# Approximate exponentials on VectorE as four shifted linear terms, in a statically ordered attention kernel

## The chip, the cores and the metric

The kernel runs on one core of a Trainium2 chip. The metric is the device time of one execution in microseconds (us). Executions of the same kernel differ by 1 to 3% here from the fastest to the slowest, mostly with the granted clock of TensorE (the share of its full speed that the profile shows as granted): a run over 1.5% above the fastest of its kernel in the same series is called slow and is left out of the ratios.

## The reference

Two attention layers read their own inputs and write side by side. Part A is multi-query attention with 32 heads of width 16, one shared key and value head, and 2048 queries and keys. Part B is a linear attention whose feature map is a pair of softmaxes over 16 values.

```python
# part A
q = (x @ wq).reshape(B, S, H, Dh)            # S = 2048, H = 32, Dh = 16
k = x @ wk;  v = x @ wv                      # one head for all
p = softmax(einsum("bhqd,bkd->bhqk", q, k) * Dh ** -0.5)
a = einsum("bhqk,bkd->bhqd", p, v) ... @ wo
# part B: phi = [softmax(pq), softmax(-pq)], kv = phi_k^T v, o = phi_q kv / (phi_q z)
return concatenate([a, b], axis=-1)          # (1, 2048, 1024), bf16
```

Part A needs 32 x 2048 x 2048 = 134 million exponentials, which is what the kernel is about.

## The kernel before

The scores are computed transposed, keys on partitions. Four heads are handled together (a head group of 512 queries: 32 such groups). A **quad** is one group against 128 keys: four 128x512 tiles of scores, one for each head. There are 32 x 16 = 512 quads. Each is turned into exponentials by one of two engines:

- ScalarE reads two or three score tiles at a time from PSUM and writes exp in bf16 (line L1620, tile `f_PT`). TensorE then multiplies a quad by the values with four matmuls that sit side by side in the array (L1662; in the trace they start 3 ns apart).
- VectorE approximates exp. It evicts each score tile as a 16-bit integer that is the bit pattern of an fp16 number near exp (L1711, `f_Z`), and refines it with two masks and two products (`f_U`, `f_E`, `f_C`). TensorE adds the three terms up with weights K: twelve matmuls (L1760).

```python
def bits():                                   # VectorE, once a tile: 128x512 f32 -> int16
    v.tensor_scalar(out=Z[:, p, h, :], in0=ps[:, bank, :], scalar1=Z1, scalar2=Z0, op0=mult, op1=add)
# ... then, once a pair of tiles (128x1024):
U = (Z & 0x3ff) | 0x3c00                      # tensor_scalar, int16
E = Z & 0x7c00                                # tensor_scalar, int16
C = Z.f16 * U.f16                             # tensor_tensor, fp16
C = C * U.f16                                 # tensor_tensor, fp16
# TensorE:  ACC += K0*V^T E + K1*V^T Z + K2*V^T C      (4 heads side by side, 3 terms)
```

The order of the instructions on every engine is fixed when the kernel is built. A greedy list scheduler keeps a clock for each engine with durations written in the program, picks the next job by priority, and emits it. VectorE gets a quad whenever its queue is short and the head group has at least `AHEAD` quads left; ScalarE gets the rest.

```python
def dq_ok(self):                              # may VectorE take another score tile?
    if self.dbusy > 3.2 or self.dz_out or (...ring of Z is full...):
        return False
    return self.dn % 4 != 0 or self.dve_quad() is not None    # a group with >= AHEAD quads left
```

Where TensorE would be idle, the scheduler inserts **filler**: matmuls with zero weights that add nothing to the accumulator (L1378). It does so while the recent activity that it reckons is under the threshold `ACTIVE`. The program uses eight banks of PSUM, the memory that TensorE writes: five for ScalarE's scores, one for the accumulator, and two that VectorE's scores and everything of part B and of the projections share.

## Time and profile before

The time before was 889.09 us (median of three runs, 889.08 to 893.94). The profiled run took 884.8 us on the core.

| engine | busy, us | idle, us | work it can't give away |
|---|---|---|---|
| ScalarE (ACT) | 819.0 | 66 | 29 us of part B |
| VectorE (DVE) | 804.9 | 80 | about 281 us: copies, part B, normalisation |
| TensorE (PE) | 818.8 | 66 | 139 us of its records are filler |

The engine line of the page (busy us, share of the span, number of instructions), and the line of the chain that ended last:

```profile
PE 818.8 (93%) x6909; PEld 256.4 (29%) x6909; DVE 804.9 (91%) x1569; ACT 819.0 (93%) x752; POOL 19.8 (2%) x48
...
DVE 64%; PE 23%; ACT 7%; DMA 2%; SPq 1%; issue 1%; POOL 0%; DVEq 0%; POOLq 0%
```

All three compute engines are busy over 90% of the span. The chain is walked back from the last instruction to whatever released it. It names VectorE most.

The groups of instructions from the page (busy us, mean ns of one | idle time just before them; "+1 forms" means that the mean mixes shapes):

```profile
L1620 ACT ACTIVATE f_PT<-f_ps 128x1536 bf16<-128x1536 f32 (+1 forms) x683 | 790.1, 1276 | 49.2 <-PE f_ps L1565 46.9
L1711 DVE TENSOR_SCALAR f_Z<-f_ps 128x512 int16<-128x512 f32 x340 | 227.9, 681 | 29.0 <-PE f_ps L1565 28.5
L1737 DVE TENSOR_TENSOR f_C<-f_C,f_U 128x1024 f16<-128x1024 f16 x170 | 114.7, 680 | 0.1
L1735 DVE TENSOR_TENSOR f_C<-f_Z,f_U 128x1024 f16<-128x1024 f16 x170 | 114.4, 681 | 0.0
L1731 DVE TENSOR_SCALAR f_U<-f_Z 128x1024 int16<-128x1024 int16 x170 | 69.1, 419 | 0.9
L1733 DVE TENSOR_SCALAR f_E<-f_Z 128x1024 int16<-128x1024 int16 x170 | 68.8, 419 | 0.0
L1662 PE MATMUL f_ps<-f_PT,f_VA 128*32 128x512 bf16 x1708 | 174.3, 399 | 3.1 <-DVE f_accS L1384 2.8
L1378 PE MATMUL f_ps<-f_ones,f_zero 128*128 128x512 bf16 (+8 forms) x493 | 139.4, 366 | 2.6 <-POOL f_ones L1398 1.9
```

340 evictions are 85 quads on VectorE; 1708 value matmuls are 427 quads on ScalarE. The last line is filler. The recorded means are longer than what an instruction costs in a stream, because neighbours overlap. Starts are in the timeline (start us, duration us):

```profile
414.30 0.42 DVE L1731 TENSOR_SCALAR f_U<-f_Z 128x1024 int16<-128x1024 int16 x1
414.64 0.42 DVE L1733 TENSOR_SCALAR f_E<-f_Z 128x1024 int16<-128x1024 int16 x1
414.98 0.68 DVE L1735 TENSOR_TENSOR f_C<-f_Z,f_U 128x1024 f16<-128x1024 f16 x1
415.58 0.68 DVE L1711 TENSOR_SCALAR f_Z<-f_ps 128x512 int16<-128x512 f32 x1
```

A mask starts 0.34 us after the one before it and an eviction 0.60 us after a product, though their records are 0.42 and 0.68 long. Sums of costs must use 0.34 and 0.60.

Busy time by stretches (us; PE, PEld, DVE, ACT, POOL, then the granted TensorE clock, DMA share, GB/s):

```profile
50.00:250.00 200.00, 186.59 (x1662) 57.79 (x1658) 196.01 (x369) 194.93 (x182) 0.00 (x0) 1.00 0.11 7
250.00:450.00 200.00, 188.97 (x1713) 58.73 (x1711) 191.71 (x360) 191.82 (x181) 6.00 (x9) 0.97 0.12 10
450.00:650.00 200.00, 186.69 (x1536) 62.48 (x1536) 194.42 (x395) 191.48 (x180) 0.00 (x0) 0.96 0.12 14
650.00:750.00 100.00, 94.73 (x777) 31.56 (x775) 94.57 (x194) 94.83 (x84) 0.00 (x0) 0.97 0.11 16
```

VectorE and ScalarE are both 95 to 98% busy from 50 to 750 us. Last, the waits of VectorE and of ScalarE before (total us, times, longest):

```profile
ACT f_PT L1620 <- PE f_ps L1565: 46.9, 70, 10.7
DVE f_Z L1711 <- PE f_ps L1565: 28.5, 33, 2.4
```

### The profile page before, as it was taken

How to read it: one execution, taken by the hardware profiler on the slowest of the kernel's cores; microseconds unless marked ns; L12 is line 12 of the kernel's file. 1: busy time of each engine (PE TensorE's matmuls, PEld its weight loads, DVE VectorE, ACT ScalarE, POOL GpSimd, SP SyncE). 2: the span in 40 equal slices, each digit the busy share in tenths (PEclk: the TensorE clock that was granted, in tenths of full speed). 3: DMA queues.
4: the chain of work that ended last, by engine and by line, in shares of the span. 5: the costliest groups of instructions: out<-in, count | busy, mean ns of one | idle time of the engine just before them, and what ended most of it. 6: DMA issues, size and time to landing. Idle time of an engine off the chain costs nothing.

```text
span 884.8 us, 16684 instructions
## 1 busy us (share of the span) xinstructions
PE 818.8 (93%) x6909; PEld 256.4 (29%) x6909; DVE 804.9 (91%) x1569; ACT 819.0 (93%) x752; POOL 19.8 (2%) x48
## 2 busy tenths in 40 slices
PE   8999998999999999999999998999999999999994
PEld 2222232323333223222233333333233322222221
DVE  4789999999999998999999999999899999788962
ACT  4999999999999999999989999999889999888982
POOL 6000000000000000002000000000000000000000
PEclk9999999999999999999889999999789999778998
DMA  6711110111111011110011102111011111111110
GB/s 141 189 14 8 7 7 3 7 8 7 8 8 17 16 7 8 7 8 5 4 8 19 7 3 42 7 8 31 2 7 22 29 8 17 27 8 7 8 7 27
DMA packets 40666, 17.05 MB, mean 19 GB/s; under 512 B 32580, under 2 KB 38212, under 8 KB 40584
## 3 DMA queue, kind: packets, MB, share of 16 engines
q1 hardware_dynamic: 40584, 15.93, 14.1%
q8 instruction: 55, 0.90, 0.4%
q14 instruction: 27, 0.22, 0.1%
HBM read 3.19 MB, written 4.19 MB: 8 GB/s over the span
## 4 chain that ended last, share of the span: by engine, by line
DVE 64%; PE 23%; ACT 7%; DMA 2%; SPq 1%; issue 1%; POOL 0%; DVEq 0%; POOLq 0%
DVE f_Z L1711 17%; DVE f_C L1735 8%; DVE f_C L1737 8%; PE f_ps L1565 8%; ACT f_PT L1620 7%; DVE f_U L1731 5%; DVE f_E L1733 4%; PE f_ps L1662 4%; PE f_ps L1378 3%; DVE f_ssum L1990 3%; PE f_ps L1760 3%; DVE f_phi L2005 3%; DVE f_qkT L1384 2%; DVE f_accS L1384 2%; DVE f_On L1803 2%; DMA f_denC<-f_accS 2%
## 5 line engine op out<-in xcount | busy, mean ns | idle before, releaser
L1620 ACT ACTIVATE f_PT<-f_ps 128x1536 bf16<-128x1536 f32 (+1 forms) x683 | 790.1, 1276 | 49.2 <-PE f_ps L1565 46.9
L1565 PE MATMUL f_ps<-f_QA,f_KR 32*128 32x512 bf16 x2048 | 348.3, 394 | 30.6 <-ACT f_PT L1620 15.9
L1711 DVE TENSOR_SCALAR f_Z<-f_ps 128x512 int16<-128x512 f32 x340 | 227.9, 681 | 29.0 <-PE f_ps L1565 28.5
L1662 PE MATMUL f_ps<-f_PT,f_VA 128*32 128x512 bf16 x1708 | 174.3, 399 | 3.1 <-DVE f_accS L1384 2.8
L1565 PEld LDWEIGHTS f_ps<-f_QA,f_KR 32*128 32x128 bf16 x2048 | 83.1, 91 | 284.6 <-ACT f_PT L1620 141.2
L1378 PE MATMUL f_ps<-f_ones,f_zero 128*128 128x512 bf16 (+8 forms) x493 | 139.4, 366 | 2.6 <-POOL f_ones L1398 1.9
L1737 DVE TENSOR_TENSOR f_C<-f_C,f_U 128x1024 f16<-128x1024 f16 x170 | 114.7, 680 | 0.1
L1735 DVE TENSOR_TENSOR f_C<-f_Z,f_U 128x1024 f16<-128x1024 f16 x170 | 114.4, 681 | 0.0
L1662 PEld LDWEIGHTS f_ps<-f_PT,f_VA 128*32 128x32 bf16 x1708 | 43.6, 93 | 114.5 <-issue 100.8
L1731 DVE TENSOR_SCALAR f_U<-f_Z 128x1024 int16<-128x1024 int16 x170 | 69.1, 419 | 0.9
L1733 DVE TENSOR_SCALAR f_E<-f_Z 128x1024 int16<-128x1024 int16 x170 | 68.8, 419 | 0.0
L1378 PEld LDWEIGHTS f_ps<-f_ones,f_zero 128*128 128x128 bf16 (+2 forms) x493 | 37.6, 98 | 68.4 <-issue 47.0
L1760 PE MATMUL f_ps<-f_E,f_VK 128*32 128x512 f16 x340 | 34.5, 396 | 4.9 <-DVE f_E L1733 2.5
L2005 DVE TENSOR_TENSOR f_phi<-f_epn,f_rs 128x1024 bf16<-128x1024 f32 x32 | 38.8, 1213 | 0.0
L1990 DVE TENSOR_REDUCE f_ssum<-f_epn 128x64 f32<-128x1024 f32 x32 | 38.6, 1208 | 0.0
L1984 ACT ACTIVATE f_epn<-f_ps 128x512 f32<-128x512 f32 x64 | 36.2, 646 | 0.9 <-PE f_ps L1975 0.8
L1943 PE MATMUL f_ps<-f_BxT,f_Bw 128*128 128x512 bf16 x128 | 34.0, 389 | 2.5 <-DVE f_QA L1384 0.7
L1555 PE MATMUL f_ps<-f_AxT,f_wq_pad 128*128 128x512 bf16 x128 | 35.2, 400 | 0.5 <-DVE f_o_sb L2084 0.4
L1760 PE MATMUL f_ps<-f_C,f_VK 128*32 128x512 f16 x340 | 33.8, 388 | 0.0
L1760 PE MATMUL f_ps<-f_Z,f_VK 128*32 128x512 f16 x340 | 33.8, 388 | 0.0
L1816 PE MATMUL f_ps<-f_wo_pad,f_On 128*128 128x512 bf16 x96 | 24.9, 382 | 0.8 <-DVE f_vaug L1384 0.5
L1384 DVE CAST f_QA<-f_ps 128x512 bf16<-128x512 f32 x32 | 21.9, 683 | 2.6 <-PE f_ps L1555 2.4
(96 smaller groups left out, 449.1 us busy)
## 6 DMA issues: line engine op xcount, KB each, us to landing
f_denS<-f_denS SPq DMA_DIRECT2D x124, 30.0 KB, 3.0
out_dram<-f_outB SPq DMA_DIRECT2D x4, 512.0 KB, 2.8
f_denC<-f_accS SPq DMA_DIRECT2D x124, 2.0 KB, 1.7
f_denS<-f_denC SPq DMA_DIRECT2D x124, 2.0 KB, 1.7
f_Bw<-in_B_wqkv_dram SPq DMA_DIRECT2D x1, 1536.0 KB, 8.0
out_dram<-f_outA SPq DMA_DIRECT2D x6, 256.0 KB, 3.0
f_outB<-in_A_wq_dram SPq DMA_DIRECT2D x1, 512.0 KB, 3.6
f_Bwo<-in_B_wo_dram SPq DMA_DIRECT2D x1, 512.0 KB, 11.5
```

The lines of the kernel that those rows point to most:

```text
L1378: mm = pe.matmul(ps[0:m, bank, 0:n], lhsT=zero[0:r, 0:m], rhs=self.ones512[0:r, 0:n], start=start, stop=start, **kw)
L1565: return pe.matmul(self.ps[:, bank, :], lhsT=self.KR[32 * g:32 * g + 32, kap * 128:(kap + 1) * 128], rhs=self.QA[32 * g:32 * g + 32, sc % ...
L1620: self.add("act", lambda a: a.activation(out=PT[:, sl[0]:sl[0] + size, :], in_=ps[:, b0:b0 + size, :], func=ACT.Exp), reads=[("PS", b0 + i ...
L1662: mm = pe.matmul(ps[32 * g:32 * g + 32, bank, :], lhsT=w, rhs=PT[:, slots[g], :], start=start, stop=stop, tile_position=(0, 32 * g))
L1711: self.add("dve", lambda v: v.tensor_scalar(out=o, in0=ps[:, bank, :], scalar1=self.Z1, scalar2=self.Z0, op0=ALU.mult, op1=ALU.add), reads ...
L1731: self.job(("dU", pair), "dve", 0.35, step(0.35, lambda v: v.tensor_scalar(out=U, in0=Z, scalar1=0x3ff, scalar2=0x3c00, op0=ALU.bitwise_an ...
L1733: self.job(("dE", pair), "dve", 0.35, step(0.35, lambda v: v.tensor_scalar(out=E, in0=Z, scalar1=0x7c00, scalar2=None, op0=ALU.bitwise_and ...
L1735: self.job(("dL", pair), "dve", 0.60, step(0.6, lambda v: v.tensor_tensor(out=C, in0=Zf, in1=Uf, op=ALU.mult), reads=zk + [("U", r)], writ ...
L1737: self.job(("dC", pair), "dve", 0.60, step(0.6, lambda v: v.tensor_tensor(out=C, in0=C, in1=Uf, op=ALU.mult), reads=[("C0", p), ("U", r)], ...
L1760: mm = pe.matmul(ps[32 * g:32 * g + 32, bank, :], lhsT=w[:, k, :], rhs=terms[k][:, p, h, :], start=start and k == 0, stop=stop and k == 2, ...
L1990: self.add("dve", lambda v: v.tensor_reduce(out=ssum[:, r, :], in_=epn[:, r, :, :].rearrange("p a (h f) -> p (a h) f", h=32), axis=AX.X, o ...
L2005: self.add("dve", lambda g: g.tensor_tensor(out=o, in0=i0, in1=i1, op=ALU.mult), reads=[("epn", r), ("epn2", r), ("rs", r)], writes=[("phi ...
```

## The change

The intent is a cheaper VectorE quad. The bit trick alone gives a piecewise-linear curve that follows 2^x with a ripple. Adding 256 to the integer multiplies by about 2^(1/4) and moves the ripple by a quarter of an octave, so four such copies, weighted by K, average the ripple out. The two masks and two products on pairs of tiles become three integer additions on a whole quad of 2048 elements, and TensorE adds four terms up instead of three.

```diff
-    K = (0.486328125, 0.49609375, 0.0810546875)
+    K = (0.353515625, 0.296875, 0.25, 0.2099609375)
-        self.Z = sb("Z", [128, self.NP, 2, 512], I16)      # + E, C of that shape, and U
+        self.Z = sb("Z", [128, self.NQ, 4, 4, 512], I16)   # ring of 3 quads x 4 terms
-        dU, dE: two masks, dL, dC: two products, for each pair of tiles
+        def shift(t):                                        # t = 1, 2, 3, for four tiles
+            v.tensor_scalar(out=Z[:, t], in0=Z[:, 0], scalar1=256.0 * t, op0=ALU.add)
-        self.job(("dpv", quad), "pe", 0.66, ...              # 12 matmuls
+        self.job(("dpv", quad), "pe", 0.87, ...              # 16 matmuls
     (cut)
-            if j.rel and s - j.rel > 5.0:                    # rank(): only released jobs age
-                p = min(p, 0.8)
+            if p > 2 and s - max(j.rel, j.since) > self.AGE: # any waiting job ages
+                p = 0.8
-    AHEAD = 7;  T_B = (54.0, 750.0)                          # part B released until 750 us
+    AHEAD = 6;  T_B = (54.0, 700.0);  NOUT = 2               # two VectorE score tiles out
     (cut)  On: 16 -> 12, pT, den, o_sb, oT: 3 -> 2, epn: 2 -> 1, output B in 16 DMAs for 4;
     filler in steps of 128 columns for 64; VectorE's queue limit (dbusy) 3.2 -> 3.0
```

The rings shrink because the four terms need 48 KB a partition where the old tiles needed 28.

## The prediction

> **What bounds it now.** The softmax of part A is 512 quads (four 128x512 key tiles each). The groups view counts 1708 value matmuls for ScalarE's quads, so ScalarE makes 427, and 340 score evictions on VectorE, so VectorE makes 85. In 150 to 750 us (busy time by stretches) VectorE is 94.6 to 99.3% and ScalarE 93.6 to 98.3% busy; over the span of 884.8 us, 804.9 and 819.0 us. They are balanced: the limit is their joint rate. (The chain of waits says VectorE 64%, ScalarE 7%; I don't read that as VectorE alone.) TensorE is 93% busy, but 139 us of its records are filler; it is slack, except where its clock is low (mean 0.961; 0.75 in 750 to 800 us). ScalarE waits 46.9 us for scores (waits view).
>
> **Removed, added, moved.** Start-to-start distances in the timeline: a 128x512 eviction 0.60 us (recorded 0.681), a 128x1024 mask 0.34 (0.419), a 128x1024 fp16 product 0.60 (0.681). A VectorE quad costs 4x0.60 + 2x(2x0.34 + 2x0.60) = 6.16 us. After: 4 evictions and 3 shifts of 2048 int16 elements. [...] New quad: 2.4 + 1.8 = 4.2 us.
>
> TensorE pays 16 value matmuls a quad for 12, about 0.21 us more (four run together in 0.21 us in the timeline), plus more single score matmuls; filler shrinks instead.
>
> **On the critical path.** All of the saving, because the greedy order moves quads to VectorE. ScalarE: 790.1/427 = 1.85 us a quad, plus 29 us features and 66 us idle. VectorE's other work: 805 - 85x6.16 = 281 us, plus 80 idle. Balance: 95 + 1.85(512 - x) = 361 + 4.2x gives x = 112.6 and T = 834 us. I add a few us because TensorE loses some 100 us of slack (42 us values, 10 single scores, 50 shorter span), so low-clock stretches should bite more. Aging of waiting jobs, two outstanding score tiles and smaller rings I count as nothing net: they allow the change rather than pay.
>
> **Predicted: 837 us, 8 in 10 between 818 and 862.** Faster by over 2%: 0.93; within 2%: 0.05; slower: 0.02.
>
> **What would show each step right or wrong.** Groups: evictions to Z about 450 (440 to 470) for 340; three shift groups, together about 340 instructions at about 0.68 us[...]. ScalarE's exponentials fall from 683 to about 640 instructions. VectorE and ScalarE stay above 93% busy in the middle. Filler records fall below 80 us. ScalarE's wait for scores stays under 80 us. Start and end stages keep their length.
>
> **What would make it wrong.** [...] (2) TensorE becomes the third bound: more switches between tilings, longer low-clock stretches, ScalarE waits over 100 us. (3) The opposite: [...]waits shrink, and it lands near 820. (4) Two PSUM banks are shared by VectorE's scores and all of part B; two score tiles out may starve part B, which then ends late and lengthens the end.

The forecast's sum came to 834 us, with 4.2 us for a new quad, and was put at 837 us with 818 to 862. The 0.60 us of a shift (so 3 x 0.60 = 1.8 us of the 4.2) was the author's estimate. From the trace before alone, two masks of 1024 (0.34 us each from start to start) for one shift would give 2.4 + 6 x 0.34 = 4.44 us a quad, and the same balance x = 108.3 and 842 us, also an estimate.

## The result, and the profile after

The kernel after took 846.5 us (median of four runs, 841.42 to 855.75); the kernel before took 890.79 us beside it. The ratio of the fast runs is 0.948 (95% interval 0.941 to 0.955). A ratio here is the mean time of one kernel's fast runs over that of the other's fast runs of the same rounds, so not quite the ratio of the medians. The kernel after was run again with the experiments (label a0_after_again): 848.58 us, ratio 0.960 (0.950 to 0.970). That ratio is higher mainly because one of the four fast runs of the kernel before in that series took only 874.85 us, at a clock of 0.983; the other ratios of section 1 share that.

The first profile of the kernel after fell in the slow state (855.75 us). Its clock column shows a peculiar thing (the third number from the end):

```profile
250.00:350.00 100.00, 94.11 (x959) 31.44 (x969) 85.54 (x143) 98.82 (x95) 0.00 (x0) 0.95 0.12 12
```

In this stretch of 100 us and the two after it the granted clock is 0.95. The clock record behind the column holds the levels 0.949 and 0.5 in this run, and 1.0 and 0.5 in that of the kernel before. So the profile of a0_after_again (mean clock 0.960, for 0.916 here) is used below as the profile after.

Page, groups and stretches of the kernel after, in the same views as before:

```profile
PE 781.0 (92%) x7279; PEld 251.0 (30%) x7279; DVE 732.4 (86%) x1295; ACT 782.6 (92%) x719; POOL 17.7 (2%) x49
...
DVE 46%; PE 35%; ACT 14%; DMA 2%; issue 1%; SPq 1%; DVEq 0%; POOL 0%; POOLq 0%
```

```profile
L1619 ACT ACTIVATE f_PT<-f_ps 128x1536 bf16<-128x1536 f32 (+2 forms) x650 | 752.9, 1262 | 48.2 <-PE f_ps L1564 43.6
L1711 DVE TENSOR_SCALAR f_Z<-f_ps 128x512 int16<-128x512 f32 x424 | 276.1, 680 | 31.0 <-PE f_ps L1564 30.7
L1724 DVE TENSOR_SCALAR f_Z<-f_Z 128x2048 int16<-128x2048 int16 x318 | 208.2, 683 | 0.6
L1661 PE MATMUL f_ps<-f_PT,f_VA 128*32 128x512 bf16 x1624 | 166.2, 400 | 4.4 <-DVE f_accS L1384 3.8
L1378 PE MATMUL f_ps<-f_ones,f_zero 128*128 128x512 bf16 (+8 forms) x247 | 74.0, 370 | 2.1 <-POOL f_zero L1397 1.3
```

```profile
50.00:250.00 200.00, 185.53 (x1753) 56.49 (x1754) 180.92 (x303) 183.91 (x169) 0.00 (x0) 0.92 0.11 7
250.00:450.00 200.00, 188.77 (x1903) 62.53 (x1901) 184.87 (x314) 195.74 (x187) 4.08 (x9) 0.98 0.11 10
450.00:650.00 200.00, 186.84 (x1660) 64.17 (x1660) 181.95 (x342) 192.53 (x181) 0.00 (x0) 0.97 0.12 16
650.00:750.00 100.00, 94.65 (x855) 29.87 (x855) 86.09 (x156) 97.76 (x86) 0.00 (x0) 0.98 0.15 19
```

Three things are to be seen (the chain still names VectorE first, with 46%, and would not have told them). The shift over 2048 elements is recorded at 683 ns, about as long as an eviction of 512 (680 ns), and the next instruction starts 0.60 us after it (median of the 318 in the profile of the first, slow run: 599 ns). VectorE made 424/4 = 106 quads and ScalarE 1624/4 = 406, so 21 quads moved. And VectorE is now less busy than before: 86% of the span, 86 to 92% in the middle, while ScalarE is at 92 to 98%. VectorE's idle time grew from 80 to 849.0 - 732.4 = 117 us. The waits of VectorE and ScalarE after:

```profile
ACT f_PT L1619 <- PE f_ps L1564: 43.6, 60, 10.1
DVE f_Z L1711 <- PE f_ps L1564: 30.7, 38, 2.8
DVE f_outA L1384 <- PE f_ps L1805: 15.5, 7, 4.8
DVE f_qkT L1384 <- PE f_ps L1932: 8.0, 8, 2.4
DVE f_ssum L1979 <- ACT f_epn L1973: 5.9, 9, 2.1
```

The wait for score tiles hardly moved (28.5 to 30.7 us). What is new is that VectorE stands in front of copies whose matmuls have not come: the output projection (15.5 us, before under 0.1), part B's projections (8.0, before 1.2), the sums of part B's features (5.9, before none). The order of VectorE's list is fixed, so a copy that is not ready holds up evictions that are. But e1b below, which is as fast, has only 1.7, 2.3 and 1.7 us of these three waits, and e1, which is slower, has 6.1, 7.2 and 5.0: they differ from order to order, and that they cost time is not shown.

### The profile page after: what moved, and what is told of

Same layout as the page of the kernel before. It is cut to its first block, busy times and chain, and to the rows that moved or that the text cites. A ratio compares the mean times of both kernels' runs of the same rounds, so it can differ in the third digit from the quotient of the medians.

```text
span 852.7 us, 17083 instructions
## 1 busy us (share of the span) xinstructions
PE 777.1 (91%) x7214; PEld 251.1 (29%) x7279; DVE 732.3 (86%) x1295; ACT 783.1 (92%) x719; POOL 17.7 (2%) x49
## 4 chain that ended last, share of the span: by engine, by line
DVE 50%; PE 35%; ACT 11%; issue 2%; DMA 1%; SPq 1%; DVEq 0%; POOL 0%; POOLq 0%
DVE f_Z L1711 19%; DVE f_Z L1724 12%; PE f_ps L1564 11%; ACT f_PT L1619 10%; PE f_ps L1749 6%; PE f_ps L1661 6%; PE f_ps L1378 3%; DVE f_ssum L1979 3%; DVE f_phi L1994 2%; PE f_ps L1932 2%; DVE f_accS L1384 2%; DVE f_QA L1384 2%; PE f_ps L1805 1%; DMA f_denC<-f_accS 1%; DVE f_On L1792 1%
## 5 line engine op out<-in xcount | busy, mean ns | idle before, releaser
L1619 ACT ACTIVATE f_PT<-f_ps 128x1536 bf16<-128x1536 f32 (+2 forms) x650 | 753.3, 1254 | 51.2 <-PE f_ps L1564 46.9
L1711 DVE TENSOR_SCALAR f_Z<-f_ps 128x512 int16<-128x512 f32 x424 | 276.5, 681 | 33.7 <-PE f_ps L1564 33.2
L1724 DVE TENSOR_SCALAR f_Z<-f_Z 128x2048 int16<-128x2048 int16 x318 | 208.3, 684 | 0.6
L1749 PE MATMUL f_ps<-f_Z,f_VK 128*32 128x512 f16 x1696 | 120.3, 407 | 1.7 <-DVE f_Z L1724 0.9
L1378 PE MATMUL f_ps<-f_ones,f_zero 128*128 128x512 bf16 (+8 forms) x247 | 74.2, 372 | 2.1 <-POOL f_zero L1397 1.3
L1749 PEld LDWEIGHTS f_ps<-f_Z,f_VK 128*32 128x32 bf16 x1696 | 39.6, 99 | 55.7 <-issue 15.8
L1378 PEld LDWEIGHTS f_ps<-f_ones,f_zero 128*128 128x128 bf16 (+2 forms) x247 | 18.8, 98 | 33.0 <-issue 20.6
L1384 DVE CAST f_qkT<-f_ps 128x512 bf16<-128x512 f32 x32 | 21.8, 683 | 5.7 <-PE f_ps L1932 5.5
L1384 DVE COPY f_accS<-f_ps 128x512 f32<-128x512 f32 x31 | 21.2, 685 | 3.4 <-PE f_ps L1661 2.6
L1792 DVE TENSOR_TENSOR f_On<-f_accS,f_denS 128x512 bf16<-128x512 f32 x31 | 21.1, 682 | 1.1 <-DMA f_denS<-f_denS 1.1
```

What stands on the lines that cost most here:

```text
L1378: mm = pe.matmul(ps[0:m, bank, 0:n].rearrange("p (a n) -> p a n", n=128), lhsT=zero[0:r, 0:m], rhs=rhs, start=start, stop=start, **kw)
L1384: self.add("dve", lambda v: v.tensor_copy(out=out, in_=in_), reads=reads, writes=writes)
L1619: self.add("act", lambda a: a.activation(out=PT[:, sl[0]:sl[0] + size, :], in_=ps[:, b0:b0 + size, :], func=ACT.Exp), reads=[("PS", b0 + i ...
L1711: self.add("dve", lambda v: v.tensor_scalar(out=o, in0=ps[:, bank, :], scalar1=self.Z1, scalar2=self.Z0, op0=ALU.mult, op1=ALU.add), reads ...
L1724: self.add("dve", lambda v: v.tensor_scalar(out=Z[:, t], in0=Z[:, 0], scalar1=256.0 * t, scalar2=None, op0=ALU.add), reads=zk, writes=[("Z ...
L1749: mm = pe.matmul(ps[32 * g:32 * g + 32, bank, :], lhsT=w[:, k, :], rhs=Zf[:, k, sl[g], :], start=start and k == 0, stop=stop and k == 3, t ...
```

## The experiments

All outputs are right. The kernel before, run beside each series, had medians of 887.8 to 888.7 us, so times can be compared across the series too.

### 1. Was it the arithmetic or the schedule?

My theory was that the cheaper arithmetic brings the gain by moving quads, and that aging, two tiles out and the rings only make room. The rival was that the new job order brings it. Four runs cross the two.

**a0_after_again**: the kernel after, unchanged.

> The kernel after, unchanged, for a profile in the fast state and as the reference of the runs beside it. Expected 838 to 850 us, ratio 0.945 to 0.955, clock above 0.96; VectorE still under 90% busy in the middle (if its low share were only the slow state's doing, it would be 93% or more).

848.58 us, clock 0.960 in the profile. The ratio is just above the expected range. VectorE's low share is no matter of the slow state.

**e1_terms_only**: the kernel before with the four terms alone, made for each pair of tiles. To find the memory, one small tile that is used at the end was laid over a dead one.

```diff
 # in the kernel before
-    dU, dE, dL, dC on a pair of tiles
+    for t in range(1, 4):                                    # 128x1024, 0.34 us each
+        v.tensor_scalar(out=Z[:, t], in0=Z[:, 0], scalar1=256.0 * t, op0=ALU.add)
+    d_pv: four terms;  K, Z0 of the kernel after
```

> The kernel before with the four-term arithmetic alone, made per pair of key tiles; old rings, old job order rules, AHEAD 7, part B released until 750 us. Theory (arithmetic pays; VectorE's quad becomes 2.4 + 6x0.34 = 4.44 us and quads move): about 97 VectorE quads, 850 to 868 us, ratio about 0.965, half of the gain or more. Rival (the schedule changes pay): within 1% of before, 880 to 895 us.

857.79 us (846.75 to 859.81), with 388/4 = 97 VectorE quads. Two of its four runs count as slow, so there is no interval for it.

**e1b_terms_ahead6**: the same with `AHEAD` 6.

> The same with AHEAD 6 (VectorE may take a quad when 6 instead of 7 quads of a head group are left). Theory: about 103 VectorE quads, 845 to 858 us, ratio about 0.955, most of the whole gain; the rest of the frame (aging, four at once, rings, two score tiles out) is then worth under 1%. Rival: those are worth more, and it stays above 860 us.

843.95 us, ratio 0.953 (0.940 to 0.967), 412/4 = 103 VectorE quads. That is the whole gain of the change with neither aging nor four tiles at once nor small rings nor two tiles out. Its VectorE is idle for 841.9 - 741.7 = 100 us.

**e2_old_terms_new_frame**: the kernel after with the old masks and products, made for four tiles at once in the new ring, and `AHEAD` 7.

> The kernel after with the old arithmetic (masks and two products, made for four key tiles at once in the new ring, three value terms), AHEAD 7; aging, small rings, two score tiles out and the earlier release of part B kept. Theory: about 93 VectorE quads of 5.87 us, no gain, 880 to 895 us, ratio 0.99 to 1.00. Rival (schedule pays): under 870 us.

890.95 us, ratio 1.011 (0.999 to 1.022), 372/4 = 93 VectorE quads. The recorded means (679 ns an eviction, 681 and 685 a mask of 2048, 1210 a product of 2048), each less the 0.08 us of overlap seen in the timeline before, give 5.86 us a quad, an estimate, for the 5.87 expected. It moved eight quads to VectorE against the kernel before and gained nothing: VectorE is 93% busy (823.6 of 884.0 us) and ScalarE acquires a wait that the kernel before had only for 0.2 us, for ring slots that value matmuls must free:

```profile
ACT f_PT L1619 <- PE f_ps L1661: 14.7, 5, 4.3
```

What follows: the arithmetic and the number of quads that the order lets VectorE take are the whole gain. The rest of the frame is worth nothing that these runs can resolve. One corner of the cross was not run: the old arithmetic with `AHEAD` 6. The scheduler alone, which needs no chip, gives it 86 quads instead of 85 and a plan that ends 6 us later by the scheduler's own clock, so it is no likely source of the gain. Aging has no run either. With no aging at all the scheduler stops with jobs left over; with the old aging rule put back in the kernel after it gives a complete order of 116 quads that ends 23 us later by its own clock. So aging may well be needed in the new frame; what it is worth on the chip is not shown.

### 2. What is the time after made of? Padding one engine at a time

VectorE's 117 us of idle time suggested that it no longer limits. To test that, some 64 us of useless work (63 to 76 as it came out) were put on one engine at a time, without telling the scheduler, so that the order stayed the same.

```diff
 # p1_pad_dve: the shift t = 3 of every quad is made twice
+                if t == 3: v.tensor_scalar(out=Z[:, t], in0=Z[:, 0], scalar1=256.0 * t, op0=ALU.add)
 # p2_pad_act: the first tile of 119 exponentials is made twice
+        if self.nex % 11 in (0, 5): a.activation(out=PT[:, sl[0], :], in_=ps[:, b0, :], func=ACT.Exp)
 # p3_pad_pe: after each of the first three terms of a quad, four matmuls with zero weights
+                        pe.matmul(ps[...], lhsT=self.zero[:, 0:32], rhs=Zf[:, k, sl[g], :], start=False, ...)
```

**p1_pad_dve**

> The kernel after, same order on every engine, with the last of the three shifts of every quad made twice: 106 x 0.60 = 64 us more on VectorE that the plan doesn't know of. The profile shows VectorE 117 us idle. Theory (VectorE is no longer the limit; ScalarE with TensorE is): the idle time absorbs most of it, +5 to +30 us over the kernel after (846 us), so 850 to 876. Rival (the chain's 50% is right, VectorE still limits): +50 to +64 us.

**p2_pad_act**

> The kernel after, with the first key tile of 118 of the 650 exponentials made a second time (about 0.54 us each, 64 us more on ScalarE). Theory (ScalarE limits): +45 to +64 us, 890 to 910. Rival (TensorE or VectorE limits): under +25 us.

**p3_pad_pe**

> The kernel after, with 12 more value matmuls of zero weights in every VectorE quad (106 x about 0.64 = 68 us more on TensorE, results unchanged). Theory (TensorE is nearly full, a third limit): +30 to +60 us, 876 to 906. Rival (TensorE has slack, filler 74 us shows it): under +15 us, perhaps with a higher granted clock.

The engine lines of the three pages, in this order:

```profile
PE 810.9 (88%) x7279; PEld 250.9 (27%) x7279; DVE 805.2 (88%) x1401; ACT 791.8 (86%) x719; POOL 18.1 (2%) x49
```

```profile
PE 793.3 (88%) x7279; PEld 251.6 (28%) x7279; DVE 741.4 (82%) x1295; ACT 845.2 (93%) x838; POOL 17.9 (2%) x49
```

```profile
PE 823.1 (93%) x8551; PEld 280.3 (32%) x8551; DVE 736.7 (83%) x1295; ACT 786.6 (89%) x719; POOL 17.8 (2%) x49
```

| run | work added (busy after it, minus 732.4, 782.6) | median, us | fast mean minus 846.8 (seven fast runs of after) | clock of the profile |
|---|---|---|---|---|
| p1_pad_dve | 805.2 - 732.4 = 73 us VectorE | 921.75 | +76 | 0.930 |
| p2_pad_act | 845.2 - 782.6 = 63 us ScalarE (0.53 us for each of the 119) | 906.97 | +62 | 0.947 |
| p3_pad_pe | about 67 us TensorE (1272/4 groups of 0.21 us, the distance in the timeline before) | 886.49 | +40 | 0.988 |

A repeat starts 0.72 us after the shift that it repeats, since it waits for that one to finish (shown under p1b; p1's own starts were not read), so by this estimate the padding took 106 x 0.72 = 76 us of VectorE's time and not 64.

My theory fell on p1: none of VectorE's idle time took the padding up. It is 920.1 - 805.2 = 115 us in p1 and was 117. The delay went to the others instead: ScalarE's wait for scores in p1 is

```profile
ACT f_PT L1619 <- PE f_ps L1564: 104.2, 132, 10.0
```

where it was 43.6 us. But the rival, that VectorE is the limit, doesn't do either, since padding ScalarE costs nearly all of what was added and TensorE costs over half. All three engines are on the path, and the chain that ended last moves to the engine that was padded: VectorE has 65% of it in p1, ScalarE 78% in p2, TensorE 57% in p3. My reading is that they hand tiles to each other through two or five PSUM banks, each in a fixed order, so that a delay on any one is passed on to the other two, and the 117 us of idle time were not spare. The number of banks was not varied, so that part is argued and not shown.

**p1b_pad_dve_planned** asks whether the fixed order was to blame: the same padding, but the scheduler knows of it.

```diff
-        self.job(("dS", quad, t), "dve", 0.60, shift(t), ...)
+        self.job(("dS", quad, t), "dve", 1.20 if t == 3 else 0.60, shift(t), ...)   # and dbusy to match
```

> As p1_pad_dve (one shift of every quad made twice, 4.8 us a quad on VectorE), but the greedy order is made with the true cost, so that it moves quads back to ScalarE: 101 VectorE quads instead of 106. Theory (the +75 us of p1_pad_dve came from delays in an order that could not answer them; the joint rate of the engines decides): my balance with 4.8 us gives 102.4 quads and 853 us, about 20 us over the same balance for 4.2 us, so 855 to 872 us. Rival (VectorE's work itself limits, whatever the order): 101 x 0.6 = 61 us less about 5 x 4.2 = 21 us, so 885 us or more.

887.01 us (884.74 to 888.15), 404/4 = 101 VectorE quads. The number of quads came as expected, the time did not: by its numbers the rival is right. Knowing of the padding took 35 of the 76 us back, not the 50 to 67 of the theory. A part of the remainder is the experiment's own: the repeated shift waits for the first one to finish, which the timeline shows.

```profile
300.88 0.68 DVE L1724 TENSOR_SCALAR f_Z<-f_Z 128x2048 int16<-128x2048 int16 x1
301.60 0.69 DVE L1727 TENSOR_SCALAR f_Z<-f_Z 128x2048 int16<-128x2048 int16 x1
302.21 0.68 DVE L1384 CAST f_QA<-f_ps 128x512 bf16<-128x512 f32 x1
```

The repeat (L1727) starts 0.72 us after the shift, where others start 0.60 apart: 101 x 0.12 = 12 us that the plan didn't have. Its runs also have a lower clock: 0.952 in the mean for 0.968 of the kernel after, worth 7 us by the slope of section 3. The plan itself ends 15 us later by the scheduler's own clock. The three add up to an estimate of 34 of the 40 us, if the 12 us show in full; the rest is not explained.

**m1_ahead3** gives VectorE more quads in the unpadded kernel.

```diff
-    AHEAD = 6
+    AHEAD = 3
```

> The kernel after with AHEAD 3 instead of 6, so that VectorE may take quads nearer the end of a head group: the order then has 114 VectorE quads, the number that my balance asked for (112.6). Theory (ScalarE waits for the accumulator and TensorE, VectorE's idle time can't be used this way): 845 to 862 us, no faster than after. Rival (only the number of quads matters, 8 x 1.85 = 15 us): 828 to 836 us.

860.15 us, ratio 0.965 (0.959 to 0.971), with 456/4 = 114 VectorE quads, the number that the prediction's balance asks for. ScalarE has 8 quads less (766.9 us busy for 782.6) and still ends later: it is idle for 26 us more, and 19 of them are a wait that the kernel after does not show at all:

```profile
ACT f_PT L1619 <- PE f_ps L1564: 45.4, 62, 10.1
ACT f_PT L1619 <- PE f_ps L1661: 19.4, 9, 5.2
```

The second line is ScalarE standing still, for up to 5.2 us at a time, until value matmuls free slots of its ring. All quads of a head group go into one accumulator, so when VectorE holds the last quads of a group, the next group's products must wait; that is read from the program. `AHEAD` is what keeps VectorE's late quads from holding up the group.

### 3. Filler and the clock

**m2_nofill** takes all filler out of the order (only the ten matmuls at the very start stay).

```diff
-    ACTIVE = 5.8
+    ACTIVE = 0.0
```

> The kernel after without filler matmuls in the order (107 VectorE quads). The prediction called filler slack. If it is only slack, the time stays within 1% of after (838 to 856 us). If it is what holds the granted clock, the clock falls under 0.93 and the time rises by 15 us or more, to 862 us or more.

899.53 us (887.29 to 904.61), ratio 1.005 (0.997 to 1.013), 428/4 = 107 VectorE quads. All that the change had won is gone, with nearly the same work on VectorE and ScalarE. The page's engine line and one stretch (clock 0.87; the next 200 us have 0.88):

```profile
PE 784.0 (88%) x6984; PEld 243.0 (27%) x7054; DVE 742.1 (84%) x1302; ACT 782.6 (88%) x717; POOL 17.9 (2%) x49
```

```profile
250.00:450.00 200.00, 179.76 (x1678) 56.12 (x1697) 174.27 (x296) 179.04 (x169) 4.16 (x9) 0.87 0.10 9
```

The mean clock is 0.877, against 0.960 in a0_after_again. If both records hold only the levels of the kernel before, 1.0 and 0.5, a quarter of the span (2 x 0.123) ran at half clock, against 8% (2 x 0.040), an estimate; in the kernel before 68.6 us, 8%, did by the record itself. So filler is not slack: it is paid work. The order is not quite the same without it, which is a rival; but by the scheduler's own clock the new order ends only 6 us later, and the measured loss is 47 us (894.2 for 846.8, means of the fast runs).

The same relation explains most of the scatter between executions. Over 85 runs of the 13 kernels, with each kernel's own mean taken off, time falls by 4.4 us for every 0.01 of mean clock (correlation -0.90). The scatter alone doesn't say which is cause and which effect; m2, where filler was taken away, is the evidence that a lower clock lengthens the run: by the slope its fall from 0.968 to 0.874 is worth 42 us, which with the 6 us of the order makes up the loss. Reduced to the clock of the kernel after (0.968) with that slope, an estimate, the three paddings cost +59, +50 and +47 us, for 76, 63 and 67 us added: 70 to 80% of each. By this estimate p3's cost was partly hidden by its higher clock (0.984 in the mean), and p1's came in part with a lower one (0.930). Whether p1's lower clock is itself an effect of the padding is not shown.

### 4. A version that beats both

If the joint rate of three engines decides, a quad that is cheaper on VectorE and on TensorE together should win more. **t3_three_terms** uses three copies, shifted by thirds of an octave; **t2_two_terms** two, half an octave apart.

```diff
-    K = (0.353515625, 0.296875, 0.25, 0.2099609375)
+    K = (0.470703125, 0.375, 0.296875);  SH = (0.0, 341.0, 683.0);  NQ = 4    # t3: 2 shifts, 12 matmuls
+    K = (0.70703125, 0.5);  SH = (0.0, 512.0);  NQ = 5;  AHEAD = 5             # t2: 1 shift, 8 matmuls
```

> Three shifted terms instead of four (shifts by thirds of an octave, 341 and 683; the ring holds four quads in the same space less): 3.6 us a quad on VectorE and 12 value matmuls instead of 16; the order has 115 VectorE quads. Theory (joint rate, TensorE in it): 22 to 30 us under after, 818 to 832 us, ratio about 0.93. Rival (after is at a floor of PSUM banks and waits that a cheaper quad doesn't lower): 838 us or more. The result should still pass: the spread of the approximate exponential around the true one is 0.2% rms against 0.11% for four terms.

> Two shifted terms (shift by half an octave), 3.0 us a quad and 8 value matmuls, AHEAD 5, a ring of five quads; the order has 123 VectorE quads. Theory: 800 to 818 us, ratio about 0.91. Spread 0.45% rms, so it may or may not pass the comparison with the reference; told as a limit, not as a proposal.

t3 took 834.73 us (five of six runs 832.06 to 835.36), ratio 0.936 (0.931 to 0.941), with 115 VectorE quads: 13 us under the kernel after by the means of the fast runs, about half of what was expected, but below the rival's floor of 838. It lowers the cost on both engines and enlarges the ring, so it does not tell which of them pays. t2 took 823.84 us, four of its six runs slow at clocks of 0.929 to 0.937; the two fast ones took 807.15 and 818.70, ratio 0.913 (0.904 to 0.921). The two agree with the expectation, the median of all six does not. The relative error of the approximate exponential, computed from the constants over scores of -6 to 6, has a spread of 0.11% rms for four terms, 0.20% for three and 0.45% for two. t3 is the version I would keep without looking again at accuracy; t2 shows where the time goes. Why its clock is low is not shown: its filler records (80 us) are no fewer than those of the kernel after (74 us).

One number was overlooked that costs no run: where the scheduler's own clock ends. Building the orders again without the chip (they come out with the numbers of quads of the runs) gives 859.8 us before and 822.2 after (38 less; measured 42 less by the fast means), 832.0 for m1 (10 more; measured 13 more), 809.5 for t3 (13 less; measured 13 less) and 827.9 for m2 (6 more; measured 47 more). The plan foretells the order's own limits better than the balance of sums does. It knows nothing of the granted clock, and m2 is where it is far off.

## Why the prediction was right or wrong

- **The size**: 837 us with 818 to 862 was predicted, and 846.5 and 848.6 us were measured. Right. A part of the hit is luck: the few us that were added to 834 for "low-clock stretches should bite more" came nearer for a reason that the runs don't bear out, since the mean clock of the fast runs was 0.962 before and 0.968 after.
- **A shift costs 0.60 us, 0.68 recorded**: right. 318 shifts at 0.683 us recorded in a0_after_again, and 0.60 us to the next start (median in the first profile of the kernel after).
- **The gain comes from moving quads, and the rest of the frame counts as nothing**: right, by e1b (0.953 without the frame) and e2 (1.011 without the arithmetic).
- **The balance**: its ScalarE side holds for the quads that ScalarE really had: 66 us idle + 29 us features + 406 x 1.85 = 846, for a span of 849.0. The step that missed is that the order would hand out quads until both engines end together. The number of quads is set when the kernel is built, and the scheduler with `AHEAD` 6 gave VectorE 106 instead of 112.6; that is 6.6 x 1.85 = 12 us more on ScalarE, which is how far the time lies above the 834 of the balance. The term "plus 80 idle" on VectorE's side then measured 117, since VectorE was given too little to fill the time. The step "VectorE and ScalarE stay above 93% busy in the middle" and the step "evictions to Z about 450" failed with it (86 to 92% for VectorE, and 424). Of the other signs, 318 shifts and 650 exponentials came near the forecast 340 and 640, and start and end kept their length (the first exponential came at 12.8 us before and 12.2 after, and 16 and 18 us follow the last one).
- **"All of the saving" is on the path**: right, but for another reason than the one written. I reasoned from two engines in balance; p1, p2 and p3 show that TensorE is a third, and that some 70 to 80% of the work added to any one of them shows in the time of the fixed order (an estimate, section 3; p1b, with a new order, got half of p1's loss back). m1 shows that the quads which the balance asked for can be given to VectorE, but the time gets worse.
- **"It is slack" of filler and TensorE**: wrong. Filler did fall as predicted (139 to 74 us of records), and ScalarE's wait for scores stayed at 43.6 us. But taking away what remains brings the mean clock from 0.968 to 0.874 and costs 47 us (m2).
- **Risk (2), TensorE as a third bound**, was named as a danger and is what the runs show, though not by the sign that I gave for it: ScalarE's waits for scores did not rise (46.9 us before, 43.6 after). What a switch between tilings costs can be read in the trace before: after a group of four value matmuls the next such group starts 0.22 us later, score matmuls 0.32 us later (medians outside the low stretches).

## What to carry to other kernels

When several engines pass small tiles to each other in a fixed order, idle time of one is no proof of slack (p1: 117 us idle, and some 73 to 76 us added cost 76): put a known amount of work on each in turn and see what the span does. A cheaper step on an engine that looks free can still pay (t3), and what then limits is in part the order itself (here the one accumulator of a head group, m1; the shared banks were not tested). Where a scheduler plans the order, ask it for its own end time before the chip. Before matmuls that compute nothing are counted as reserve, one run should show what the clock does without them (m2: 0.968 to 0.874).

## What the traces show of the clock and of VectorE's starts

- In the kernel before the clock record falls from 1.0 to 0.5 at 433.9 us of the span and is back at 447.6. TensorE was working: there is no gap over 0.90 us in its records in the 6 us ahead, and of the 47 matmuls that started in those 6 us, 39 use a quarter of the array's rows or columns (32 of 128). Groups of four value matmuls go from 0.22 to 0.40 and 0.43 us apart in the lines below. What made the clock fall is not shown.

```profile
429.53 0.40 PE L1760 MATMUL f_ps<-f_E,f_VK 128*32 128x512 f16 x4 [0.23 <-DVE f_E L1733]
429.75 0.39 PE L1760 MATMUL f_ps<-f_Z,f_VK 128*32 128x512 f16 x4
...
432.24 0.39 PE L1565 MATMUL f_ps<-f_QA,f_KR 32*128 32x512 bf16 x3 [0.90 <-ACT f_PT L1620]
...
434.45 0.62 PE L1760 MATMUL f_ps<-f_E,f_VK 128*32 128x512 f16 x4
434.85 0.64 PE L1760 MATMUL f_ps<-f_Z,f_VK 128*32 128x512 f16 x4
435.28 0.64 PE L1760 MATMUL f_ps<-f_C,f_VK 128*32 128x512 f16 x4
```

- The slow run of the kernel after, on one core, sat at 0.949 between its low stretches. The matmuls bear a slower clock out, if not its exact level: full-array matmuls of 512 columns in a row start 224 ns apart in that run and 216 in the kernel before (medians outside the low stretches).
- The clock record and the matmuls agree: in the low stretches of the kernel before the same matmuls start 426 ns apart (median of 17), for the 216 outside.
- In p1b a shift of 2048 that waits for the one just ahead of it starts 0.72 us after that one, where others start 0.60 apart.
- The recorded duration of a shift of 2048, 683 ns, is not what the stream pays for it: starts are 0.60 us apart (kernel after).
